# Attention, a gated FFN and an eight-expert block in one kernel: one expert's 264 rows computed with stationary weights, and score masks in quadrants

## The chip, the core and the metric

The kernel runs on one core of one Trainium2 chip. Its time is the device time of a launch in microseconds, as the median of several runs. The engines are TensorE (PE, with its weight loads as PEld), VectorE (DVE), ScalarE (ACT), GpSimd (POOL) and SyncE (SP), whose queue starts most transfers.

## What is computed

The reference, cut to what matters:

```python
# q, k, v: (4, 8, 576, 64); window 64
scores = scale * q @ k.T;  mask = (0 <= i - j < 64);  attn = softmax(where(mask, scores, -1e9))
x = attn @ v                                             # 2304 tokens x 512
x = x / sqrt(mean(x * x) + 1e-6) * rms_g
x = (silu(x @ w_gate) * (x @ w_val)) @ w_out             # 512 -> 1536 -> 512
e = argmax(x @ r_gate);  gate_w = softmax(x @ r_gate)[e];  eom = sigmoid(x @ r_eom)
out = gate_w * eom[e] * (relu(x @ w1[e]) @ w2[e])        # 8 experts, 512 -> 1024 -> 512
```

Every fp32 product outside attention is made of three products of rounded parts: high by high, high by low, low by high (`hi_i` and `lo_i` split an operand; the data type is fp32r). So a product over 512 inputs is 4 x 3 = 12 matmuls, and one over 1024 inputs is 24.

## The kernel before

**Stages.** Attention runs over 18 tiles of 128 tokens (`attention_tile`). The FFN runs over 7 parts of two or three tiles in 6 groups (`SIZES`, `GROUPS`); each group goes through the 24 slices of the hidden size, gate, value and output product (L999 to L1001, L1041 to L1043). `route` finds each token's expert and scatters its row into a table in DRAM, in which every expert has a range of its own. `experts` then runs nine blocks: a first block of 256 rows for the expert that leads before the last FFN part is done, then eight blocks, the experts in order of their number of tokens, with as many rows as `CAPS` says. What is over is left to a loop (`moe_rest`), whose number of turns is computed on the chip.

**One expert block.** `tokens` loads 128 rows at a time and transposes them (L1475). `weights` loads the expert's weights in eight parts of 512 KB into a buffer `raw` (six of these) and splits them into high and low parts (`w`). `wide` makes the first product: eight slices of the hidden size, each 12 matmuls with the weights stationary and the block's rows moving (L1544 to L1546), then relu and split (`eh`, L1550 to L1555). `block` makes the second product: for each tile of 128 rows, 24 matmuls with the hidden values stationary and 512 columns of weights moving (L1578 to L1580), so the rows come out as rows; a tile with 64 rows makes as many matmuls. The result is scaled by the token's factor (`osb`, L1589, L1591) and scattered to the output by POOL (L1596).

**The scores of one tile.** For each half j of the heads there is a result bank. A mask is laid into it first, by one matmul of `both_b` (two identities side by side) with `masks`, 512 columns (L680). A query of 64 positions looks at the 64 keys before its own and its own 64, so the mask has one triangle for each. A query that begins a sequence (4 of 36) has nothing before it: a second matmul of 256 columns adds the full mask there (L687). Then 32 matmuls of 64 x 64 add the scores (L694).

**The order of the work.** Every operation is given to a planner (`Plan`) with its cost on each engine it could run on, its buffers and a due time. `Plan.order` simulates the engines and writes one order for all of them; `SHIFT` is a list of corrections to the due times, and `K` holds the planner's settings: `SW`, the cost counted when TensorE changes between small tiles (`tiled=True`) and the whole array; `stk`, how far such work is preferred while the array is in small tiles; `warm`, until when result bank 7 of 8 is kept for filler matmuls, which keep TensorE busy in the start (L625); `vb`, `vb2` and `share`, the choice between engines. The lines in question are these:

```python
first = min((x for x in ready[e] if x[2].tiled and not x[2].done), default=None)
if first is not None and first[0] < min(x[0] for x in ready[e]) + K["stk"]:
    ...
pl.tags["bank"][7]["free"] = K["warm"]
```

Of the kernel before, what the change touches and what calls it, by code (L numbers as in the profile page):

```python
# [22 lines left out]
P = 128  # L23
# [10 lines left out]
CAPS = [128, 448, 384, 320, 256, 256, 256, 192]  # L34
SW = 0.165
# [3 lines left out]
    w_r=4, sl=1.2, n_q=4, n_kt=4, n_s=4, n_m=4, n_p=4, n_x=4, n_y=3, n_xf=1, n_val=3, pf=0.1, cold=6.0, late=1, f0=24.0, pw=110.0, pb=0.6, c1a=0, c1v=0, spe=4, lact=0, warm=38.762, wf=2.97, flead=24.233, nwv=1, port=1.0, t0=46.214, pp=93.267,  # L39
    lead=1.781, clead=9.978, stag=2.552, stage=1.001, slack=0.136, nt=2, look=-0.104, marg=-0.509, dw=1.843, ewl=3.278,  # L40
    ews=8.339, xld=43.407, xtn=7.222, mlead=14.712, vb=0.41, vb2=-0.81, tb=1165.45, share=0.149, pls=9, phs=9, sf=0, hfs=1.431, stk=305.664, rlead=7.936, span=0.317, wl=1.841,
# [46 lines left out]
]  # L88


class Buf:


    def __init__(self, tag=None, t=None):
        self.tag, self.t, self.slot = tag, t, None
# [279 lines left out]
def attention_ffn_moe(  # L375
# [291 lines left out]
    def attention_tile(t, qt, kt, al):  # L667
# [4 lines left out]
        def half(j):  # L672
            return slice(64 * j, 64 * j + 64)
# [1103 lines left out]
```

## Time and profile before

| | |
|---|---|
| median of 3 runs | 822.24 us (822.12 to 823.24) |
| the profiled execution's own time | 820.1 us |
| its span, first to last instruction | 818.4 us |
| TensorE busy | 803.6 us, 98% |
| VectorE, ScalarE, POOL busy | 473.7, 353.9, 70.2 us |
| granted TensorE clock, mean | 0.998 of full speed |

The span is what the trace covers; the time of a launch has 1.7 us around it in this execution. A matmul's busy time reaches from its start to its result, and the next one starts before that end, so the distance between two starts is what a matmul costs in a dense stretch.

### The profile page before, as it was taken

Reading aid. Unit: us, or ns where it says so; the run is one execution under the profiler, and the core shown is the slowest. Engines: PE = TensorE matmul, PEld = TensorE weight load, DVE = VectorE, ACT = ScalarE, POOL = GpSimd, SP = SyncE. Lnnn points to the kernel's source line nnn. Section 1 sums busy time; section 2 is a strip of 40 time slices with the busy share of each in tenths; the row PEclk is TensorE's granted clock in tenths of the full one; section 3 lists DMA queues with packets and bytes.
Section 4 is the critical chain, followed back from the end, with each engine's and each line's share of the span. In section 5 each row is a group of like instructions: output and inputs, shape, how many; then the busy total and the mean of one; then the engine's idle time right before and its main releaser. Section 6 shows DMA issues by size and latency. Waiting matters only on the chain.

```text
span 818.4 us, 15636 instructions
## 1 busy us (share of the span) xinstructions
PE 803.6 (98%) x5954; PEld 723.4 (88%) x5954; DVE 473.7 (58%) x1246; ACT 353.9 (43%) x990; POOL 70.2 (9%) x131
## 2 busy tenths in 40 slices
PE   9999999999999999999999999999999999999995
PEld 8888999989999898899899998899788798889993
DVE  6999999557553534632553224453465576767740
ACT  6898777547432424421642121223243323344430
POOL 2210001021101000200021001000200010111100
PEclk9999999999999999999999999999999999999999
DMA  8797979968325502632129506600594653756600
GB/s 317 260 331 246 336 291 315 297 229 314 115 104 202 191 1 68 224 124 88 52 105 356 196 2 195 228 1 1 148 291 146 215 173 121 244 165 207 205 27 20
DMA packets 54012, 146.34 MB, mean 179 GB/s; under 512 B 6800, under 2 KB 6800, under 8 KB 53936
## 3 DMA queue, kind: packets, MB, share of 16 engines
q1 hardware_dynamic: 50912, 135.48, 48.8%
q0 software_dynamic: 3024, 9.85, 3.1%
q8 instruction: 47, 0.77, 0.4%
q14 instruction: 29, 0.24, 0.1%
HBM read 120.77 MB, written 24.54 MB: 178 GB/s over the span
## 4 chain that ended last, share of the span: by engine, by line
PE 79%; issue 8%; DMA 8%; DVE 3%; ACT 1%; POOL 1%; SPq 0%; POOLq 0%; DVEq 0%
PE bank L999 12%; PE bank L1001 12%; PE bank L1000 12%; PE bank L1041 6%; PE bank L1042 6%; PE bank L1043 6%; DMA out_dram<-osb,meta 5%; PE bank L1544 2%; PE bank L1546 2%; PE bank L1545 2%; PE bank L1579 2%; PE bank L1580 2%; PE bank L1578 2%; PE bank L774 2%; PE bank L694 2%
## 5 line engine op out<-in xcount | busy, mean ns | idle before, releaser
L999 PE MATMUL bank<-xn,w 128*128 128x384 f32 (+1 forms) x672 | 215.5, 321 | 0.7 <-DVE u L1016 0.7
L1001 PE MATMUL bank<-xn,w 128*128 128x384 f32 (+1 forms) x672 | 210.4, 313 | 0.0
L1000 PE MATMUL bank<-xn,w 128*128 128x384 f32 (+1 forms) x672 | 210.3, 313 | 0.0
L999 PEld LDWEIGHTS bank<-xn,w 128*128 128x128 f32 x672 | 127.2, 189 | 5.0 <-DVE u L1016 1.0
L1000 PEld LDWEIGHTS bank<-xn,w 128*128 128x128 f32 x672 | 127.2, 189 | 1.6
L1001 PEld LDWEIGHTS bank<-xn,w 128*128 128x128 f32 x672 | 127.1, 189 | 0.0
L459 DVE TENSOR_TENSOR w<-raw,w 128x512 fp32r<-128x512 f32 x128 | 82.4, 684 | 7.4 <-ACT w L452 7.0
L1041 PE MATMUL bank<-wo,h 128*128 128x512 f32 x216 | 86.0, 398 | 0.0
L1043 PE MATMUL bank<-wo,h 128*128 128x512 f32 x216 | 84.9, 393 | 0.0
L1042 PE MATMUL bank<-wo,h 128*128 128x512 f32 x216 | 84.9, 393 | 0.0
L1016 DVE SCALAR_TENSOR_TENSOR u<-u,bank 128x384 f32<-128x384 f32 (+1 forms) x84 | 41.5, 494 | 66.8 <-ACT u L1011 66.3
L1011 ACT ACTIVATE u<-bank 128x384 f32<-128x384 f32 (+1 forms) x84 | 37.5, 446 | 94.9 <-PE bank L1001 94.0
L452 ACT CAST h<-u 128x384 fp32r<-128x384 f32 (+1 forms) x75 | 35.1, 468 | 96.4 <-DVE u L1024 96.3
L1024 DVE TENSOR_TENSOR u<-u,bank 128x384 f32<-128x384 f32 (+1 forms) x84 | 41.5, 494 | 57.8 <-PE bank L1001 57.0
L452 ACT CAST w<-raw 128x512 fp32r<-128x512 f32 x81 | 47.4, 619 | 54.8 <-DMA raw<-in_moe_w_dram 36.2
L1544 PE MATMUL bank<-xT,w 128*128 128x256 f32 (+4 forms) x224 | 68.4, 305 | 0.0
L1545 PE MATMUL bank<-xT,w 128*128 128x256 f32 (+4 forms) x224 | 68.1, 304 | 0.0
L1546 PE MATMUL bank<-xT,w 128*128 128x256 f32 (+4 forms) x224 | 68.1, 304 | 0.0
L1578 PE MATMUL bank<-w,eh 128*128 128x512 f32 (+1 forms) x168 | 66.6, 397 | 0.0
L1579 PE MATMUL bank<-w,eh 128*128 128x512 f32 (+1 forms) x168 | 66.2, 394 | 0.0
L1580 PE MATMUL bank<-w,eh 128*128 128x512 f32 (+1 forms) x168 | 66.2, 394 | 0.0
L1550 ACT ACTIVATE eh<-bank 128x256 fp32r<-128x256 f32 (+4 forms) x61 | 25.6, 420 | 68.7 <-PE bank L1546 66.6
(234 smaller groups left out, 1332.2 us busy)
## 6 DMA issues: line engine op xcount, KB each, us to landing
w<-whd SPq DMA_DIRECT2D x80, 512.0 KB, 4.5
raw<-in_moe_w_dram SPq DMA_DIRECT2D x64, 512.0 KB, 4.8
whd<-w SPq DMA_DIRECT2D x24, 512.0 KB, 5.5
val<-in_v_dram SPq DMA_DIRECT2D x18, 512.0 KB, 5.6
kt<-in_k_dram SPq DMA_DIRECT2D x18, 384.0 KB, 5.5
raw<-in_moe_w_gate_dram SPq DMA_DIRECT2D x12, 512.0 KB, 5.1
raw<-in_moe_w_val_dram SPq DMA_DIRECT2D x12, 512.0 KB, 4.0
raw<-in_moe_w_out_dram SPq DMA_DIRECT2D x12, 512.0 KB, 5.1
```

Source lines behind the costliest of these rows:

```text
L999: nc.tensor.matmul(o, lhsT=h_, rhs=xn.t[:, 0, kk], start=(kk == 0), stop=False)
L1000: nc.tensor.matmul(o, lhsT=h_, rhs=xn.t[:, 1, kk], start=False, stop=False)
L1001: nc.tensor.matmul(o, lhsT=l_, rhs=xn.t[:, 0, kk], start=False, stop=(kk == KD - 1))
L1041: nc.tensor.matmul(o, lhsT=h.t[:, 0, c], rhs=wo.t[:, 0, f], start=(n == 0), stop=False)
L1042: nc.tensor.matmul(o, lhsT=h.t[:, 0, c], rhs=wo.t[:, 1, f], start=False, stop=False)
L1043: nc.tensor.matmul(o, lhsT=h.t[:, 1, c], rhs=wo.t[:, 0, f], start=False, stop=(n == NF - 1))
L1544: nc.tensor.matmul(o, lhsT=wh, rhs=x.t[:, 0, kk, 0:N], start=(kk == 0), stop=False)
L1545: nc.tensor.matmul(o, lhsT=wh, rhs=x.t[:, 1, kk, 0:N], start=False, stop=False)
L1546: nc.tensor.matmul(o, lhsT=wl, rhs=x.t[:, 0, kk, 0:N], start=False, stop=(kk == KD - 1))
L1578: nc.tensor.matmul(bk.t[0:M], lhsT=hh, rhs=wh, start=(f == 0), stop=False)
L1579: nc.tensor.matmul(bk.t[0:M], lhsT=hh, rhs=wl, start=False, stop=False)
L1580: nc.tensor.matmul(bk.t[0:M], lhsT=hl, rhs=wh, start=False, stop=(f == NF2 - 1))
```

## The change

The block of the fourth expert in order has 264 rows, not 320. A block whose last tile has at most 32 rows (here 8) now makes its second product the other way round (`turned_block`): the weights are stationary, 128 output columns at a time, and all the block's rows move. The four results are copied out of their banks as columns by rows (into one buffer `raw` and one `t2k`), and four transposes for each tile of rows turn them back; then they are scaled and scattered as before (`weighted`, the old code as a function). The score mask is now four matmuls of 64 x 64 weights and 512 columns, one for each half of the heads and each half of the queries, and a query that begins a sequence takes its mask from other columns of `masks`, so the extra matmul is gone. The planner's settings and the whole `SHIFT` list are new.

```diff
-CAPS = [128, 448, 384, 320, 256, 256, 256, 192]
-SW = 0.165
+CAPS = [128, 448, 384, 264, 256, 256, 256, 192]
+SW = 0.06
...
-    ... warm=38.762, wf=2.97, ... slack=0.136, look=-0.104, marg=-0.509, dw=1.843, vb=0.41, vb2=-0.81, tb=1165.45, share=0.149, stk=305.664
+    ... warm=62.816, wf=1.644, ... slack=-0.04, look=-0.072, marg=-0.199, dw=1.739, vb=0.333, vb2=0.243, tb=22.485, share=-0.055, stk=0.0
...
 SHIFT = [
-    -22.3, 22, -5.8, 15.9, 30.3, 28.9, 11.1, 7.3, 39.4, -27.8, -41.3, -28, ...
...
-    both_b = fixed("both_b", [P, P], BF16)
+    both_b = fixed("both_b", [P, 64], BF16)
...
         def mmc(e):
-            for j, bk in enumerate(col):
-                nc.tensor.matmul(
-                    bk.t.rearrange("p (i g w) -> p i g w", i=4, g=2), lhsT=both_b.t[half(j)],
-                    rhs=masks.t[half(j), 0:2].unsqueeze(1).to_broadcast([64, 4, 2, 64]), start=True, stop=False,
-                )
             for c in range(2):
                 for j, bk in enumerate(col):
-                    if st[c]:
-                        nc.tensor.matmul(
-                            bk.t[half(c)].rearrange("p (i g w) -> p i g w", i=4, g=2)[:, :, 0], lhsT=both_b.t[half(j), 0:64],
-                            rhs=masks.t[half(j), 2].unsqueeze(1).to_broadcast([64, 4, 64]), start=False, stop=False,
-                        )
+                    nc.tensor.matmul(
+                        bk.t[half(c)].rearrange("p (i g w) -> p i g w", i=4, g=2), lhsT=both_b.t[half(j)],
+                        rhs=masks.t[half(j), slice(0, 3, 2) if st[c] else slice(1, 3)].unsqueeze(1).to_broadcast([64, 4, 2, 64]),
+                        start=True, stop=False,
+                    )
...
-            {"t": 1.4 + 0.3 * any(st)}, mmc, r=[qt, kt, both_b, masks], w=col, hold=halves, prio=pr + 2 * sg, tiled=True
+            {"t": 1.28}, mmc, r=[qt, kt, both_b, masks], w=col, hold=halves, prio=pr + 2 * sg, tiled=True
...
+    def turned_block(b, w, N, hs, pr):
+        yb = [Buf("raw"), Buf("t2k")]
+        def y(d):
+            return yb[0].t[:, d * N:d * N + N].bitcast(F32) if d < 3 else yb[1].t[:, 0:N]
+        for d in range(KD):
+            bk = bank()
+            for g in range(2):
+                def mm2(e, d=d, g=g, bk=bk):
+                    for f in range(4 * g, 4 * g + 4):
+                        t = ew[w, 2 + f // 4, f % 4 // 2].t
+                        wh, wl = (t[:, z, f % 2].rearrange("p k f -> p (k f)")[:, d * P:(d + 1) * P] for z in range(2))
+                        hh, hl = (hs[f][0].t[:, z, 0:N] for z in range(2))
+                        o = bk.t[:, 0:N]
+                        nc.tensor.matmul(o, lhsT=wh, rhs=hh, start=(f == 0), stop=False)
+                        nc.tensor.matmul(o, lhsT=wh, rhs=hl, start=False, stop=False)
+                        nc.tensor.matmul(o, lhsT=wl, rhs=hh, start=False, stop=(f == NF2 - 1))
+                pl.op({"t": 12 * mmt(N) + 0.02}, mm2, ..., w=[bk], prio=pr)
+                pr += 12 * mmt(N)
+            pl.op(cost(N, "hp"), lambda e, d=d, bk=bk: hi_i(e, y(d), bk.t[:, 0:N]), r=[bk], w=[(yb[d // 3], d)], prio=pr)
+        for j in range(-(-N // P)):
+            bk = bank()
+            M = min(P, N - j * P)
+            def back(e, j=j, bk=bk, M=M):
+                for d in range(KD):
+                    nc.tensor.transpose(bk.t[0:M, d * P:(d + 1) * P], y(d)[:, j * P:j * P + M], ident.t)
+            pl.op({"t": 0.43}, back, r=[*yb, ident], w=[bk], prio=pr + 0.5, rows=0.5)
+            weighted(b, j, M, bk, pr + 0.5)
+        return pr
...
     def block(b, w, N, pr):
         hs = narrow(b, w, pr) if N == P else wide(b, w, N, pr)
         pr += 6.5 if N == P else NF2 * 12 * mmt(N)
+        if 0 < N % P <= 32:
+            return turned_block(b, w, N, hs, pr)
```

## Rows read from the trace of the kernel before

**Rows 1.** The page's part 1: busy time, share of the span, instructions.

```profile
PE 803.6 (98%) x5954; PEld 723.4 (88%) x5954; DVE 473.7 (58%) x1246; ACT 353.9 (43%) x990; POOL 70.2 (9%) x131
```

**Rows 2.** Busy time by stretch: start:end, length, engines, clock, DMA share, GB/s.

```profile
core 0: us, PE busy (x) PEld busy (x) DVE busy (x) ACT busy (x) POOL busy (x), PEclk, DMA share, GB/s
0.00:20.00 20.00, 18.45 (x312) 16.00 (x313) 12.46 (x40) 12.43 (x59) 4.84 (x31) 1.00 0.88 315
40.00:60.00 20.00, 19.69 (x202) 17.82 (x199) 19.55 (x53) 19.43 (x57) 2.08 (x2) 1.00 0.91 334
560.00:600.00 40.00, 37.63 (x250) 32.19 (x249) 17.28 (x77) 13.34 (x31) 5.08 (x7) 1.00 0.43 129
677.50:726.50 49.00, 49.00 (x291) 42.95 (x290) 31.99 (x69) 18.35 (x36) 5.10 (x5) 1.00 0.56 179
```

**Rows 3.** The same for the filler matmuls alone (L625), until 41.4 us.

```profile
0.00:41.40 41.40, 16.48 (x216) 14.97 (x216) 1.00 0.81 289
```

**Rows 4.** What TensorE waited for: us in total, times, longest.

```profile
PE bank L1475 <- DMA t2k<-xs: 1.6, 1, 1.6
...
PE bank L1475 <- DMA xs<-xs: 0.7, 2, 0.4
```

**Rows 5.** Timeline of TensorE, expert stage: start, busy time, instruction; stretches of one width.

```profile
682.53 0.31 PE L1544 MATMUL bank<-xT,w 128*128 128x320 f32 x1
...
686.06 0.40 PE L1578 MATMUL bank<-w,eh 128*128 128x512 f32 x1
...
688.86 0.31 PE L1544 MATMUL bank<-xT,w 128*128 128x320 f32 x1
...
738.95 0.28 PE L1545 MATMUL bank<-xT,w 128*128 128x256 f32 x1
...
744.51 0.39 PE L1578 MATMUL bank<-w,eh 128*128 128x512 f32 x1
...
784.83 0.28 PE L1545 MATMUL bank<-xT,w 128*128 128x192 f32 x1
...
787.40 0.42 PE L1578 MATMUL bank<-w,eh 128*128 128x512 f32 x1
```

**Rows 6.** The same timeline: four transposes, and the matmul behind them.

```profile
677.53 0.60 PE L1475 MATMUL bank<-ident,xs 128*128 128x128 f32 x4
677.88 0.39 PE L1544 MATMUL bank<-xT,w 128*128 128x320 f32 x1
```

**Rows 7.** Groups of instructions by shape: evictions behind the first product.

```profile
L1550 ACT ACTIVATE eh<-bank 128x256 fp32r<-128x256 f32 x29 | 11.2, 385 | 25.0 <-PE bank L1546 23.7 <-PE bank L1280 1.2
L1550 ACT ACTIVATE eh<-bank 128x320 fp32r<-128x320 f32 x8 | 3.5, 438 | 12.2 <-PE bank L1546 12.1
...
L1555 DVE SCALAR_TENSOR_TENSOR eh<-bank,eh 128x256 fp32r<-128x256 f32 x32 | 13.2, 420 | 11.8 <-ACT eh L1550 11.7
```

**Rows 8.** The page's part 6: loads of expert weights, KB, us to landing.

```profile
raw<-in_moe_w_dram SPq DMA_DIRECT2D x64, 512.0 KB, 4.8
```

**Rows 9.** Timeline of TensorE: two score groups; the first begins a sequence.

```profile
28.91 0.39 PE L680 MATMUL bank<-masks,both_b 64*128 64x512 bf16 x2
...
30.33 0.32 PE L851 MATMUL bank<-ident,y 128*128 128x128 f32 x1
...
75.13 0.39 PE L1043 MATMUL bank<-wo,h 128*128 128x512 f32 x1
75.45 0.39 PE L680 MATMUL bank<-masks,both_b 64*128 64x512 bf16 x2
75.77 1.10 PE L694 MATMUL bank<-kt,q 64*64 64x128 f32 x32
76.81 0.39 PE L999 MATMUL bank<-xn,w 128*128 128x256 f32 x1
77.03 0.28 PE L1000 MATMUL bank<-xn,w 128*128 128x256 f32 x1
```

**Rows 10.** Timeline of TensorE between the last FFN matmul and the first big block.

```profile
564.21 0.39 PE L1043 MATMUL bank<-wo,h 128*128 128x512 f32 x1
...
592.37 0.66 PE L1475 MATMUL bank<-ident,t2k 128*128 128x128 f32 x4 [1.62 <-DMA t2k<-xs]
```

More of the change, by code (lines that the diff above doesn't have):

```diff
@@ L38 @@
 K = dict(
-    w_r=4, sl=1.2, n_q=4, n_kt=4, n_s=4, n_m=4, n_p=4, n_x=4, n_y=3, n_xf=1, n_val=3, pf=0.1, cold=6.0, late=1, f0=24.0, pw=110.0, pb=0.6, c1a=0, c1v=0, spe=4, lact=0, warm=38.762, wf=2.97, flead=24.233, nwv=1, port=1.0, t0=46.214, pp=93.267,
-    lead=1.781, clead=9.978, stag=2.552, stage=1.001, slack=0.136, nt=2, look=-0.104, marg=-0.509, dw=1.843, ewl=3.278,
-    ews=8.339, xld=43.407, xtn=7.222, mlead=14.712, vb=0.41, vb2=-0.81, tb=1165.45, share=0.149, pls=9, phs=9, sf=0, hfs=1.431, stk=305.664, rlead=7.936, span=0.317, wl=1.841,
+    w_r=4, sl=1.2, n_q=4, n_kt=4, n_s=4, n_m=4, n_p=4, n_x=4, n_y=3, n_xf=1, n_val=3, pf=0.1, cold=6.0, late=1, f0=24.0, pw=110.0, pb=0.6, c1a=0, c1v=0, spe=4, lact=0, warm=62.816, wf=1.644, flead=24.233, nwv=1, port=1.0, t0=46.214, pp=93.267,
+    lead=1.781, clead=9.978, stag=2.552, stage=1.001, slack=-0.04, nt=2, look=-0.072, marg=-0.199, dw=1.739, ewl=3.278,
+    ews=8.339, xld=43.407, xtn=7.222, mlead=14.712, vb=0.333, vb2=0.243, tb=22.485, share=-0.055, pls=9, phs=9, sf=0, hfs=1.431, stk=0.0, rlead=7.936, span=0.317, wl=1.841,
 )
 SHIFT = [
[42 rows of a table removed]
[42 rows of a table added]
 ]
@@ L518, in c_masks @@
             r = slice(64 * c, 64 * c + 64)
-            a = masks.t[r, 0]
+            a = masks.t[r, 1]
             nc.gpsimd.affine_select(
@@ L522, in c_masks @@
             )
-            a = masks.t[r, 1]
+            a = masks.t[r, 2]
             nc.gpsimd.affine_select(
@@ L529, in c_zero @@
         nc.vector.memset(ident.t, 0.0)
-        nc.vector.memset(masks.t[:, 0:2], 0.0)
-        nc.vector.memset(masks.t[:, 2], NEG)
+        nc.vector.memset(masks.t[:, 1:3], 0.0)
+        nc.vector.memset(masks.t[:, 0], NEG)
     def c_ones(e):
@@ L548, in c_both @@
     def c_both(e):
-        nc.vector.tensor_tensor(out=both_b.t[:, 0:64], in0=ident.t[:, 0:64], in1=ident.t[:, 64:P], op=ALU.add)
-        nc.vector.tensor_tensor(out=both_b.t[:, 64:P], in0=ident.t[:, 0:64], in1=ident.t[:, 64:P], op=ALU.add)
-    pl.op({"v": 0.28}, c_both, r=[ident], w=[both_b], prio=-97)
+        nc.vector.tensor_tensor(out=both_b.t, in0=ident.t[:, 0:64], in1=ident.t[:, 64:P], op=ALU.add)
+    pl.op({"v": 0.14}, c_both, r=[ident], w=[both_b], prio=-97)
     made = pl.op({"v": 0.4}, c_ones, w=[ones, ones_b, tri, seed_b], prio=-98)
@@ L1563, in wide @@
         return hs
+    def turned_block(b, w, N, hs, pr):
[14 more added lines that the diff above has]
+                        nc.tensor.matmul(o, lhsT=wl, rhs=hh, start=False, stop=(f == NF2 - 1))
+                pl.op(
+                    {"t": 12 * mmt(N) + 0.02}, mm2, r=[ew[w, 2 + g, hf] for hf in range(2)] + [h for h, _ in hs[4 * g:4 * g + 4]],
+                    w=[bk], prio=pr,
+                )
+                pr += 12 * mmt(N)
[9 more added lines that the diff above has]
+        return pr
@@ new lines, in weighted, with scaled, put @@
+    def weighted(b, j, M, bk, pr):
+        o, m = Buf("osb"), meta[b, j]
+        def scaled(e):
+            if e == "a":
+                nc.scalar.activation(out=o.t[0:M], in_=bk.t[0:M], func=AF.Copy, scale=m.t[0:M, 1:2])
+            else:
+                nc.vector.tensor_scalar(out=o.t[0:M], in0=bk.t[0:M], scalar1=m.t[0:M, 1:2], scalar2=None, op0=ALU.mult)
+        def put(e):
+            nc.gpsimd.indirect_dma_start(
+                out=out, out_offset=bass.IndirectOffsetOnAxis(ap=m.t[0:M, 0:1].bitcast(I32), axis=0),
+                in_=o.t[0:M], in_offset=None, bounds_check=NT - 1, oob_is_err=False,
+            )
+        pl.op({"a": 0.55, "v": 0.61}, scaled, r=[bk, m], w=[o], prio=pr)
+        puts.append(pl.op({"p": 1.0}, put, r=[o, m], dma=0.73, prio=pr, after=puts[-1:]))
@@ L1584, in block @@
                 pr += 2.78
-            o, m = Buf("osb"), meta[b, j]
-            def scaled(e, bk=bk, o=o, m=m, M=M):
-                if e == "a":
-                    nc.scalar.activation(out=o.t[0:M], in_=bk.t[0:M], func=AF.Copy, scale=m.t[0:M, 1:2])
-                else:
-                    nc.vector.tensor_scalar(
-                        out=o.t[0:M], in0=bk.t[0:M], scalar1=m.t[0:M, 1:2], scalar2=None, op0=ALU.mult
-                    )
-            def put(e, o=o, m=m, M=M):
-                nc.gpsimd.indirect_dma_start(
-                    out=out, out_offset=bass.IndirectOffsetOnAxis(ap=m.t[0:M, 0:1].bitcast(I32), axis=0),
-                    in_=o.t[0:M], in_offset=None, bounds_check=NT - 1, oob_is_err=False,
-                )
-            pl.op({"a": 0.55, "v": 0.61}, scaled, r=[bk, m], w=[o], prio=pr)
-            puts.append(pl.op({"p": 1.0}, put, r=[o, m], dma=0.73, prio=pr, after=puts[-1:]))
+            weighted(b, j, M, bk, pr)
         return pr
@@ L1612, in experts @@
             todo.append((b, w, n, at, at + NF2 * c1))
-            at += NF2 * c1 + -(-n // P) * 2 * 2.78
+            at += NF2 * c1 + (8 * 12 * mmt(n) + 1.3 if 0 < n % P <= 32 else -(-n // P) * 2 * 2.78)
         done_w = set()
```

84 rows, old and new, of the table SHIFT are left out of this document.

## The prediction

> **What bounds the kernel now.** I read the busy shares first, then the stretches, then what TensorE waited for, and last its instructions in order of time. TensorE is busy 98% of the span, VectorE 58%, ScalarE 43%, and it has a weight load for every matmul [rows 1]. But a matmul's busy time runs past the start of the next one, so I judge by start-to-start distances. By stretches: in the first 20 us TensorE has gaps and shares the time with 216 filler matmuls that end before 41.4 us [rows 2, 3]; from 40 to 60 us it is nearly gapless, with VectorE at 19.55 and ScalarE at 19.43 of 20 us; from 560 to 600 us it lacks 2.4 us; in the 49 us around the block that is changed it has no gap at a granted clock of 1.00, while VectorE is busy 32 us and ScalarE 18 [rows 2]. All waits that the trace gives to TensorE's matmuls in the expert stage are 1.6 + 0.7 us, for the loads behind the last scatter [rows 4]. So after the start the time is the sum of TensorE's start-to-start distances, and what is taken from that sum in the expert stage comes off the end.
>
> **The block of 264 rows: first product.** It stays 8 x 12 = 96 matmuls, with 264 moving columns for 320. At 320 columns, 24 matmuls start between 682.53 and 686.06 us, 0.147 us each; at 512, 12 between 686.06 and 688.86, 0.233 each; at 256, 47 between 738.95 and 744.51, 0.118 each; at 192, 23 between 784.83 and 787.40, 0.112 each [rows 5]. From 256 to 320 that is 0.00045 us a column, so 264 columns give an estimated 0.122 us; the bounds are 0.118 (as 256) and 0.147 (as 320), and 264 is nearest to 256. Saved: 96 x (0.147 - 0.122) = 2.4 us (0 to 2.8).
>
> **Second product, turned.** Removed: three token tiles of 24 matmuls with 512 columns; the last of them holds 64 rows and costs as much as a full one. 72 x 0.233 = 16.8 us. Added: four column tiles of the output, 24 matmuls each, 264 columns, with the weights stationary: 96 x 0.122 = 11.7 us (11.3 to 14.1). Each matmul has its own weight load before and after; that load is of the kind that the 256-column rows already carry. Added too: the way back, three groups of four transposes. Such a group takes 0.35 us, and the matmul behind it starts late by 0.24 - 0.147 = 0.09 us [rows 6], so 0.44 us a group, 1.3 us in all. The last group has 8 rows and may be cheaper; I leave it at that. Net: 16.8 - 11.7 - 1.3 = 3.8 us saved (1.4 to 4.2).
>
> **What goes beside it.** Four evictions of 264 columns are new. The nearest rows are 0.385 us on ScalarE and 0.420 on VectorE for 256 columns [rows 7]: 1.7 us in all. The eight pairs of evictions after the first product shrink from 0.438 us at 320 columns (ScalarE's half) towards 0.385, 0.4 us on either engine. Both engines have over 15 of 49 us free there [rows 2], so this costs nothing as long as the transposes back are queued behind another block's matmuls; if they are not, the last eviction is bare, about 0.5 us. The turned output takes one of six buffers into which weights are loaded, and one of the two small ones, for some 10 us. Weight parts come one in 2.8 us (eight to a block of 256 rows, 96 x 0.118 + 48 x 0.233 = 22.5 us), and land in 4.8 us [rows 8]; five buffers then allow 14 us a part, landing included. The scatters keep their count, three, and POOL does little else there (5.1 us of 49).
>
> **Masks in quadrants.** Before, a tile's mask takes two matmuls, each on 64 rows and 128 columns of the array, and the 32 score matmuls behind them use tiles of 64 x 64. In the steady stage the mask starts at 75.45 us, the scores at 75.77, the next work at 76.81 [rows 9]: 0.32 us for the mask, though one matmul of 512 columns paces at 0.233. So about 0.1 us is lost where the tile's shape changes. A like amount is lost going in (75.13 + 0.233 against 75.45) and coming out (0.22 to the second matmul against 0.118). After, the four mask matmuls have the scores' shape. If the four run at once, as the scores do (32 matmuls in 1.04 us, 0.033 each, where a whole-array matmul of as many fp32 columns takes 0.35 / 4 = 0.088 [rows 6, 9]), the change of shape between mask and scores goes: 0.1 us a tile. The Trainium skill (TensorEngine Tiling (Array Packing), Key Properties) says that a change of tiling mode, not of tile, drains the engine; the 0.32 us agrees, and by that rule one drain of three goes at each tile. The four tiles that begin a sequence also lose their extra matmuls: mask and scores take 1.42 us there (28.91 to 30.33) for 1.36, so 0.06 us each [rows 9]. Four of the 18 tiles run in the start, where fillers take up what is saved. I take 14 x 0.1 + 3 x 0.06 = 1.6 us. Below that nothing may come (the drain stays); the worst case is a rival. At the head, one VectorE instruction less is hidden behind the first loads.
>
> **The new plan.** All due times change, so the order on every engine does. One setting is plain: work in small tiles is no longer preferred when the array is in that mode. Two such groups back to back save the way out and in, 0.19 us; at most 9 pairs, so 0 to 1.7 us lost; I take 0.5. The last of TensorE's eight result banks is kept for fillers until 62.8 us of the plan, for 38.8; see the rivals. Otherwise I count the plan at zero, both signs open.
>
> **Sum.** 820.1 us of the profiled execution - 2.4 - 3.8 - 1.6 + 0.5 = 812.8 us. The median of the runs, 822.24, lies 2.1 us above that execution, so 814.9 for the median. A difference under 0.2% (1.6 us) is about what this kernel's runs can't tell from none. The forecast's own range, from the bounds: 812.5 to 819.
>
> **Rivals.**
> 1. *The plan gives part back* (16%). Two places. The last FFN matmul starts at 564.21 and the first tokens of the big blocks reach TensorE at 592.37; in between only the first block of 256 rows (22.5 us) and the last routing cover, and 2.4 us stay bare already [rows 2, 10]. Whatever of that block is ordered earlier opens the wait by as much. And with a bank fewer from 38.8 to 62.8 us, where four banks hold sums and four are left for all else, up to a quarter of 24 us = 6 us could go. Typical: 3 us, 818; with 6 us, 821. Against it: the planner counts banks and waits itself, and this stretch is bound by VectorE and ScalarE as well [rows 2]. Only above 7.3 us does it turn the sign.
> 2. *The plan also gains* (10%): the 2.4 us at 590 and some of the 16.5 us of fillers before 41.4 us [rows 3, 4] go. 811 to 812.
> 3. *The four masks run one after another* (4%): slower. Place: the score group of 18 tiles. Four at 0.233 are 0.93 us for 0.32, so 0.61 x 18 = 11 us lost against 6.2 - 0.5 saved: about 827.5. It decides the sign from 0.32 us a tile on. For it: no row here has four such matmuls of 512 columns. Against it: the score rows, whose matmuls would take 2.8 us if whole-array pacing held, and take 1.04 [rows 6, 9].
> 4. *Narrow matmuls pay a fixed price* (4%): between 192 and 256 columns the distance moves by only 0.006 us, so below some width the columns no longer set it. If that held 264 at 0.147, the block would save 16.8 - 14.1 - 1.3 = 1.4 us and the sum be 819.7. Against it: the row at 256 columns, on the near side, paces at 0.118 [rows 5]. The Trainium skill (TensorE: Matmul & The Clock Gate, Back-to-back issue gap) speaks against the change: it gives a sustained 81 ns a matmul at 128 columns and 131 at 512. By a line between these (an estimate from that page) 264 columns take 0.099 us, 96 matmuls 9.5 us against 9.4 for the 72 removed, and the turned product loses the 1.3 us of transposes; the rows disagree, with 0.118 at 256 and 0.233 at 512 [rows 5].
> 5. *The block does not hold its tokens* (2%): were there more than 264, the loop that follows the planned part would run once: eight weight parts that land in 4.8 us each [rows 8], two buffers deep, 19 us or more, so 834 and up. The reference's inputs send 258 tokens to that expert by my count, and none of that loop's matmuls shows before, so only a miscount would do it.
>
> **Chances.** Forecast 64%, rivals 16, 10, 4, 4, 2. Faster by over 0.2%: 64 + 10 + 10 of the first rival + 2 of the fourth = 86%; within 0.2%: 3 + 2 = 5%; slower: 3 of the first rival, 4 and 2 = 9%. Range 810.5 to 819.5: it takes the forecast's range, the second rival and the lighter half of the first, and leaves out the rest, some 2 in 10.
>
> **What would show it.** Right: matmuls of 264 columns 0.12 to 0.125 us apart in both products; four groups of 24 in the turned one, three groups of transposes at 0.35 to 0.45 us; four mask matmuls starting together and the scores 0.2 to 0.25 us behind them; TensorE's last matmul some 7 us earlier in the span, and the same work behind it. Wrong: a gap of over 3 us between the last FFN matmul and the big blocks; TensorE waiting at 40 to 63 us or for turned results; more fillers behind 41 us; a mask of over 0.3 us; a matmul from the loop behind the planned part.

## The result, and the profile after

| | before | after |
|---|---|---|
| median of the runs | 822.22 us (822.12 to 823.24) | 814.68 us (812.85 to 816.35) |
| the profiled execution: time, span | 820.1, 818.4 us | 815.9, 813.9 us |
| TensorE's last matmul starts | 809.15 us | 804.60 us |

The ratio of the medians is 0.9905 (0.9878 to 0.9932). The forecast was 814.9 us. A second measurement of the same kernel, in five rounds, gave 814.15 us and 0.9902 (0.9885 to 0.992); its profiled execution took 815.3 us. So the median fell by some 8 us, while the profiled executions lie only 4 to 5 us apart: the one of before is near the fast end of its runs, both of after lie above the medians of theirs. What a part is worth is read below from medians, and from traces only stretch by stretch.

The page of the kernel after, part 1, as in [rows 1]:

```profile
PE 798.6 (98%) x6050; PEld 723.1 (89%) x6050; DVE 471.1 (58%) x1262; ACT 355.0 (44%) x993; POOL 59.6 (7%) x103
```

Busy time by stretch (columns as in [rows 2]) and what TensorE waited for, as in [rows 4]:

```profile
40.00:60.00 20.00, 19.97 (x192) 18.66 (x193) 19.33 (x49) 17.42 (x56) 1.77 (x2) 1.00 0.84 282
560.00:600.00 40.00, 39.43 (x264) 33.92 (x263) 19.55 (x79) 13.46 (x32) 5.04 (x7) 1.00 0.38 124
677.00:725.00 48.00, 46.53 (x342) 43.71 (x342) 27.00 (x62) 20.76 (x44) 5.47 (x5) 1.00 0.53 174
```

```profile
PE bank L1538 <- DVE eh L1549: 1.5, 2, 1.1
PE bank L993 <- DVE u L1010: 1.3, 1, 1.3
...
PE bank L1591 <- DVE eh L1549: 0.4, 1, 0.4
...
PE bank L1469 <- DMA xs<-xs: 0.2, 1, 0.2
```

The reader sees what moved. Of the 2.4 us that TensorE lacked from 560 to 600 us in [rows 2], 0.6 is left, and the waits for the scatter's loads (now L1469) have shrunk to 0.2 us. In their place stand 1.3 us at the end of the FFN (L993; 0.7 us before), 1.5 us behind the changed block, where before there was no gap, and 0.45 us at 773 us, two blocks on. The TensorE timeline of the changed block:

```profile
693.98 0.28 PE L1538 MATMUL bank<-xT,w 128*128 128x264 f32 x1
...
699.74 1.47 PE L1469 MATMUL bank<-ident,xs 128*128 128x128 f32 x12
700.97 0.37 PE L1575 MATMUL bank<-eh,w 128*128 128x264 f32 x1
...
709.83 0.28 PE L1538 MATMUL bank<-xT,w 128*128 128x256 f32 x1
...
712.67 0.49 PE L1591 MATMUL bank<-ident,raw 128*128 128x128 f32 x3
...
713.64 0.55 PE L1591 MATMUL bank<-ident,raw 128*128 128x128 f32 x3 [0.38 <-DVE eh L1549]
...
714.58 0.39 PE L1538 MATMUL bank<-xT,w 128*128 128x256 f32 x1
...
722.86 0.39 PE L1632 MATMUL bank<-w,eh 128*128 128x512 f32 x1
724.34 0.39 PE L1538 MATMUL bank<-xT,w 128*128 128x256 f32 x1 [1.09 <-DVE eh L1549]
```

48 matmuls of the first product in 5.76 us, 0.120 each; 72 of the turned one from 700.97 to 709.83, 0.123 each, for 0.149 at 320 columns and 0.232 for the 512 columns that they replace. The transposes back begin 24 matmuls behind the turned product, so the copies out are covered, and take 1.9 us to 714.58 with a wait of 0.38 in between.

A score group of after (answering [rows 9]), and a pair of groups of before that [rows 9] does not show:

```profile
255.45 0.41 PE L680 MATMUL bank<-masks,both_b 64*64 64x512 bf16 x4
255.69 1.04 PE L688 MATMUL bank<-kt,q 64*64 64x128 f32 x32
256.67 0.45 PE L993 MATMUL bank<-xn,w 128*128 128x384 f32 x1
```

```profile
388.64 0.34 PE L1001 MATMUL bank<-xn,w 128*128 128x384 f32 x1
388.91 0.39 PE L680 MATMUL bank<-masks,both_b 64*128 64x512 bf16 x2
...
390.27 0.39 PE L680 MATMUL bank<-masks,both_b 64*128 64x512 bf16 x2
...
391.62 0.50 PE L1041 MATMUL bank<-wo,h 128*128 128x512 f32 x1
391.95 0.39 PE L1042 MATMUL bank<-wo,h 128*128 128x512 f32 x1
```

The scores start 0.24 us behind the masks, for 0.32, and a group takes 1.22 us, for 1.36; the tiles that begin a sequence take 1.21 too, for 1.42. Two groups back to back took 2.71 us before, twice 1.355; what lies in front of them and behind them they pay once and not twice (below).

### The profile page after: what moved, and what is told of

Read it like the earlier page. It is cut to its first block, busy times and chain, and to the rows that moved or that the text cites. A ratio compares the mean times of both kernels' runs of the same rounds, so it can differ in the third digit from the quotient of the medians.

```text
span 813.9 us, 15811 instructions
## 1 busy us (share of the span) xinstructions
PE 798.6 (98%) x6050; PEld 723.1 (89%) x6050; DVE 471.1 (58%) x1262; ACT 355.0 (44%) x993; POOL 59.6 (7%) x103
## 4 chain that ended last, share of the span: by engine, by line
PE 78%; issue 9%; DMA 6%; DVE 4%; SPq 1%; ACT 1%; POOL 0%; POOLq 0%; ACTq 0%; DVEq 0%
PE bank L993 11%; PE bank L995 10%; PE bank L994 10%; PE bank L1035 5%; PE bank L1036 5%; PE bank L1037 5%; PE bank L1538 3%; PE bank L1540 3%; PE bank L1539 3%; DMA raw<-in_moe_w_dram 3%; PE bank L1630 3%; PE bank L1632 3%; PE bank L1631 3%; PE bank L768 2%; PE bank L751 2%
## 5 line engine op out<-in xcount | busy, mean ns | idle before, releaser
L993 PE MATMUL bank<-xn,w 128*128 128x384 f32 (+1 forms) x672 | 215.2, 320 | 1.3 <-DVE u L1010 1.3
L994 PE MATMUL bank<-xn,w 128*128 128x384 f32 (+1 forms) x672 | 210.1, 313 | 0.0
L993 PEld LDWEIGHTS bank<-xn,w 128*128 128x128 f32 x672 | 127.2, 189 | 6.2 <-DVE u L1010 1.7
L1010 DVE SCALAR_TENSOR_TENSOR u<-u,bank 128x384 f32<-128x384 f32 (+1 forms) x84 | 41.4, 494 | 88.4 <-ACT u L1005 88.0
L1538 PE MATMUL bank<-xT,w 128*128 128x256 f32 (+4 forms) x224 | 68.0, 304 | 1.5 <-DVE eh L1549 1.5
L1540 PE MATMUL bank<-xT,w 128*128 128x256 f32 (+4 forms) x224 | 67.3, 300 | 0.0
L1539 PE MATMUL bank<-xT,w 128*128 128x256 f32 (+4 forms) x224 | 67.2, 300 | 0.0
L1630 PE MATMUL bank<-w,eh 128*128 128x512 f32 (+1 forms) x144 | 57.3, 398 | 0.0
L1632 PE MATMUL bank<-w,eh 128*128 128x512 f32 (+1 forms) x144 | 56.7, 394 | 0.0
L1631 PE MATMUL bank<-w,eh 128*128 128x512 f32 (+1 forms) x144 | 56.7, 394 | 0.0
```

What stands on the lines that cost most here:

```text
L993: nc.tensor.matmul(o, lhsT=h_, rhs=xn.t[:, 0, kk], start=(kk == 0), stop=False)
L994: nc.tensor.matmul(o, lhsT=h_, rhs=xn.t[:, 1, kk], start=False, stop=False)
L1538: nc.tensor.matmul(o, lhsT=wh, rhs=x.t[:, 0, kk, 0:N], start=(kk == 0), stop=False)
L1539: nc.tensor.matmul(o, lhsT=wh, rhs=x.t[:, 1, kk, 0:N], start=False, stop=False)
L1540: nc.tensor.matmul(o, lhsT=wl, rhs=x.t[:, 0, kk, 0:N], start=False, stop=(kk == KD - 1))
L1630: nc.tensor.matmul(bk.t[0:M], lhsT=hh, rhs=wh, start=(f == 0), stop=False)
```

## The experiments

Medians are of each kernel's runs; ratios are to the kernel before on the same chip (822.55, 821.6 and 822.62 us in the three sessions). A kernel "in the order of before" gives every engine the instruction order of before (with the turned block, up to that block: there and just behind it some evictions and weight splits change place or engine), so its stretches can be compared one by one.

**The block alone**: `CAPS` with 264, `turned_block` and `weighted`, in the code of before, settings, corrections and the due times of all other work kept.

```diff
-CAPS = [128, 448, 384, 320, 256, 256, 256, 192]
+CAPS = [128, 448, 384, 264, 256, 256, 256, 192]
+        if 0 < N % P <= 32:
+            return turned_block(b, w, N, hs, pr)
```

> The kernel before with the block part alone: 264 rows, turned second product; masks, settings and due-time corrections of before, and all due times of the other blocks kept. Theory A: the 6.2 us of the block come off, so 816 (815 to 817.5). Theory B (the new plan made the gain, the turned block loses by bare evictions and by the buffer it takes from the weight loads): 819.5 to 823.

815.04 us (814.15 to 816.22), 0.9915 (0.9898 to 0.9931). So 7.0 us (5.7 to 8.4), and no TensorE wait behind 593 us: the forecast 6.2 is within.

**The rows alone**: 264 rows in the code of before, nothing turned, planned as if they were 320.

```diff
-CAPS = [128, 448, 384, 320, 256, 256, 256, 192]
+CAPS = [128, 448, 384, 264, 256, 256, 256, 192]
+        PN = 320 if b == 3 else N
-            pl.op(cost(N, "hp"), relu, r=[bk], w=[(h, 0)], prio=pr)
+            pl.op(cost(PN, "hp"), relu, r=[bk], w=[(h, 0)], prio=pr)
```

> The kernel before with 264 rows for 320 in the fourth expert's block, nothing turned, its order unchanged. Theory (a matmul of 264 columns paces at 0.120 to 0.122 us, one of 320 at 0.147): 96 x 0.026 = 2.5 us, so 819.7 beside 822.2. Rival (the whole gain of the block, 7 us with the turn, comes from the turn): no change, 822.

818.37 us (817.29 to 820.67), 0.9959 (0.9946 to 0.9973): 3.4 us (2.2 to 4.4): the 2.5 of the pace lies within, nothing does not. The turn takes the rest of the 7.0, 3.6 us.

**The masks alone**: `c_masks`, `c_both` and the mask matmuls of after in the code and the order of before.

```diff
-                    bk.t.rearrange("p (i g w) -> p i g w", i=4, g=2), lhsT=both_b.t[half(j)],
-                    rhs=masks.t[half(j), 0:2].unsqueeze(1).to_broadcast([64, 4, 2, 64]), start=True, stop=False,
+                        bk.t[half(c)].rearrange("p (i g w) -> p i g w", i=4, g=2), lhsT=both_b.t[half(j)],
+                        rhs=masks.t[half(j), slice(0, 3, 2) if st[c] else slice(1, 3)].unsqueeze(1).to_broadcast([64, 4, 2, 64]),
```

> The kernel before with the four-quadrant masks alone, and the planner's cost for the group left at its old number, so that the order of all work is that of before. Theory A (one change of tile shape goes at each tile): 0.1 us in each of the 14 tiles behind the start and a little for the tiles that begin a sequence, 1.4 to 2.0 us, so about 820.5. Rival (the change of shape is paid elsewhere): no change, 822. Rival (the four run one after another): 827 and more.

818.72 us (817.51 to 822.47), 0.9963 (0.9946 to 0.9979): 3.0 us (1.7 to 4.4), above theory A's 1.4 to 2.0, which the interval still reaches. The timeline of the pair in this kernel:

```profile
277.02 0.34 PE L995 MATMUL bank<-xn,w 128*128 128x384 f32 x1
277.29 0.41 PE L680 MATMUL bank<-masks,both_b 64*64 64x512 bf16 x4
...
278.41 0.39 PE L680 MATMUL bank<-masks,both_b 64*64 64x512 bf16 x4
...
279.60 0.50 PE L1035 MATMUL bank<-wo,h 128*128 128x512 f32 x1
279.93 0.39 PE L1036 MATMUL bank<-wo,h 128*128 128x512 f32 x1
```

2.31 us for the pair: 1.12 and 1.19, 0.1 us less than twice the 1.21 of a group alone. With the masks of before the pair took no less than twice a group.

**The masks back**: the changed kernel, order unchanged, with the masks of before.

```diff
-                        bk.t[half(c)].rearrange("p (i g w) -> p i g w", i=4, g=2), lhsT=both_b.t[half(j)],
+                    bk.t.rearrange("p (i g w) -> p i g w", i=4, g=2), lhsT=both_b.t[half(j)],
+                    rhs=masks.t[half(j), 0:2].unsqueeze(1).to_broadcast([64, 4, 2, 64]), start=True, stop=False,
```

> The changed kernel with the masks of before (two matmuls of 512 columns, and the extra one for tiles that begin a sequence), planner's cost unchanged, so that the order of all work is that of the changed kernel. Theory A, with the mask term as the run in the order of before measured it (3 us, where the forecast had 1.6 to 2): 817 to 818, that is 0.994 of the kernel before. Rival (that run's 3 us came from something else, the group itself gives 0.1 us a tile): 815.5 to 816.

817.76 us (817.04 to 820.82), 0.995 (0.9933 to 0.9966), beside 0.9902 for the changed kernel: 3.9 us for the masks, as theory A has it; the two intervals leave 1 to 7.

**The plan alone**: the code of before, 320 rows and old masks, with the settings and corrections of after.

```diff
-SW = 0.165
+SW = 0.06
-K = dict(..., warm=38.762, ..., stk=305.664, ...)
+K = dict(..., warm=62.816, ..., stk=0.0, ...)
```

> The kernel before (320 rows, second product not turned, masks of before) with the planner's settings and due-time corrections of the changed kernel. Theory A (the plan is worth nothing by itself): 821 to 824. Theory C (the new plan gives 2 us back that the two code parts had earned): 824 to 826. Theory B (the new plan gains by itself): 817 to 820.

823.39 us (822.88 to 825.48), 1.0026 (1.0011 to 1.004): 2.1 us slower, and within the range of theory A.

**The changed code under the old plan**: settings and corrections of before, due times as in the block's experiment, the new cost of a mask.

> The changed kernel with the planner's settings and due-time corrections of before, and the due times of the other blocks as before: both code parts, not the new plan. Theory A (the plan is worth nothing by itself): 814 to 815.5, as the changed kernel. Theory B (the new plan is needed for the gain): 817 or more. Theory C (the new plan gives a part back): 812 to 814.

818.34 us (815.93 to 819.34), 0.9952 (0.9933 to 0.9971): theory B by its number, which the next run does not bear out.

**Both parts in the order of before**: the block's kernel above with the new masks, at the masks' old cost.

> The block part in the plan of before, and the new masks in the same order, the planner's cost for the group left at its old number. If the two parts add up as measured alone (7.0 and 3.0 us): 812 to 813, 0.988 of before, and the new plan gives some 2 us back. If they do not add up (as with the settings of before and the new cost, 818): 815 or more, and the masks' gain is lost elsewhere once the block is shorter.

814.74 us (814.3 to 815.25), 0.9911 (0.9882 to 0.994), the same as the changed kernel. The parts measured alone would make 10 us, this run gives 7.3 (4.9 to 9.7). Beside the one before it here, this kernel has the same code, planned with another cost for the mask. The order of the work, the engine of some operations (VectorE 1244 instructions for 1249, ScalarE 995 for 999) and the number of fillers (216 for 252) follow from that; the medians lie 3.6 us apart, though the intervals overlap a little.

**An own buffer for the turned result**, in place of `raw`, in the changed kernel.

```diff
-        yb = [Buf("raw"), Buf("t2k")]
+        yb = [Buf("yy"), Buf("t2k")]
```

> The changed kernel with a buffer of its own for the turned output, not one of the six that weights are loaded into; the planner orders the work anew around it. If the taken buffer makes the next block's weights late (TensorE waits 1.5 to 1.9 us behind the turned block, for relu results that stand behind weight splits): those waits go, 812 to 813. Rival (the waits come from the order, not from the buffer): they stay or move, 814 to 816.

815.16 us (812.99 to 817.0), 0.9913 (0.9885 to 0.9942): no gain that shows. In its trace the next weight load starts at 708.34 us, not at 713.28 as in the changed kernel, so the buffer does seem to hold loads back, but TensorE still waits 0.67 us at the transposes and 0.53 at 770 us (0.38 and 0.45 in the changed kernel). The same execution lost some 1.6 us to the clock in the FFN (last section), so its whole time says little about the buffer.

**Bank 7 free early**, in the changed kernel.

```diff
-K = dict(..., warm=62.816, ...)
+K = dict(..., warm=38.762, ...)
```

> The changed kernel with result bank 7 free at 38.8 us of the plan, as before, not at 62.8. The order follows from the planner and so moves elsewhere too. The prediction's theory (a bank counts for little there): within 1 us of the changed kernel's 814.2 to 814.7. Rival: the 38 fillers that now lie between 40 and 62.8 us (2.6 us busy) stand in for work that found no bank; then 811.5 to 812.

817.52 us (817.04 to 817.85), 0.9946 (0.9927 to 0.9965): some 3 us slower, against both expectations. The fillers of the changed kernel, then of this one (in bank 7, and in other banks), with first and last start:

```profile
L624 PE MATMUL warm<-ones_b x248: 219/219/314, 1.2 to 44.1; 128*128 128x128 bf16 x124
```

```profile
L624 PE MATMUL warm<-ones_b x206: 218/219/312, 1.2 to 39.6; 128*128 128x128 bf16 x103
L624 PE MATMUL bank<-ones_b x48: 219/219/231, 41.8 to 94.7; 128*128 128x128 bf16 x48
```

With the bank free, fillers went on in the other banks, 254 in all for 248. So this run changes the order and leaves the fillers, and does not price the bank by itself. TensorE waits 2.6 us for `u` (L993) and 1.3 for `x` (L680) here, where the changed kernel waited 1.3 for `u` and not for `x`.

**Not turned**: the changed kernel with the second product of before, 264 rows, corrections kept for all other work.

```diff
-        if 0 < N % P <= 32:
-            return turned_block(b, w, N, hs, pr)
```

> The changed kernel with its second product not turned: three tiles of 24 matmuls with 512 columns as before, 264 rows, the corrections to the due times kept for all other work. Theory: the turn saves 16.8 - 11.7 - 1.3 = 3.8 us, so 818.0 to 818.5 beside the changed kernel's 814.2 to 814.7. Rival: the 1.5 us that TensorE waits around the turned product and the 3 us of transposes with what is bare behind them eat most of it: under 1.5 us, 815.7.

816.23 us (815.68 to 817.97), 0.9929 (0.991 to 0.9948). In medians the turn is worth 2.2 us here, between the two expectations and just clear of noise. From the last transposes of `t2k` (L1469 of after) to the last matmul the traces show 217.3 us for 214.9, 2.4 us; without TensorE's waits in that stretch, 1.2 and 2.1 us, it is 3.4. So the turn itself keeps most of its worth, and the changed kernel has 0.9 us more of waits.

**Five sizes narrowed**, on the kernel with both parts in the order of before.

```diff
-CAPS = [128, 448, 384, 264, 256, 256, 256, 192]
+CAPS = [128, 440, 376, 264, 240, 240, 232, 192]
+PLANNED = {440: 448, 376: 384, 240: 256, 232: 256}
```

> The block and the masks in the order of before, with seven sizes narrowed on top: 448 to 440 rows, 384 to 376, 256 to 240 twice and 256 to 232, each block planned with its old width, so the order stands. Only the first products get narrower: 96 matmuls for each size. Theory that the columns set the pace at every width (0.00045 us a column between 256 and 320): 72 columns x 96 = 6912, times 0.00045 = 3.1 us off the 814.7 of both parts in the old order, so 811.6. Rival, a floor under some width: between 192 and 256 the distance moves by 0.0001 us a column, so the three narrow sizes give 56 x 96 x 0.0001 = 0.5 us and the two wide ones 0.7, 1.2 us in all: 813.5.

810.6 us (810.05 to 810.95), 0.9859 (0.9834 to 0.9884): better than both kernels, 4 us below the one that it starts from and past both expectations. (The text counts seven sizes; those it lists are five.) Its TensorE timeline, 36 matmuls of 240 columns and then 36 of 232:

```profile
745.79 0.27 PE L1542 MATMUL bank<-xT,w 128*128 128x240 f32 x1
...
749.84 0.27 PE L1542 MATMUL bank<-xT,w 128*128 128x232 f32 x1
...
753.86 0.40 PE L1634 MATMUL bank<-w,eh 128*128 128x512 f32 x1
```

0.1125 and 0.1117 us each. Over the whole stage the mean start-to-start distances are 0.111 at 192 columns, 0.112 at 232, 0.114 at 240, 0.1187 at 256, 0.173 at 376, 0.175 at 384, 0.201 at 440, 0.205 at 448. So the five sizes save 96 x (0.004 + 0.002 + 2 x 0.0045 + 0.007) = 2.1 us. Of the rest, the profiled executions show 2.9 us as waits and a slow stretch of its parent's that this kernel has not to that extent (below), against 1.0 us of new waits for `eh`.

## Why the prediction came out right, point by point

**The block: right, place and size.** In kernels with the order of before, the time from TensorE's last transposes of `t2k` (L1475 of before) to its last matmul is one and the same work but for the edit (with the masks, their gain lies ahead of it):

| order of before, with | last transposes of `t2k` | last matmul | between |
|---|---|---|---|
| nothing (before) | 592.8 | 809.15 | 216.4 |
| 264 rows | 592.3 | 806.34 | 214.1 |
| 264 rows, turned | 593.1 | 803.20 | 210.1 |
| masks | 590.6 | 808.17 | 217.6 |
| masks, 264 rows, turned | 591.5 | 804.15 | 212.6 |
| the same, five sizes narrowed | 590.3 | 799.79 | 209.5 |

The rows give 2.3 us (forecast 2.4), the turn 4.0 (forecast 3.8); without the waits in the first three stretches (0.8, 0.6 and 0.2 us) they give 2.2 and 3.5. Rival 4, a fixed price that would hold 264 columns at 0.147, is refuted by the 0.120 to 0.124; a floor exists, but lower: 0.111 at 192 columns and 0.112 at 232. The Trainium skill's figures for a sustained matmul (TensorE: Matmul & The Clock Gate, Back-to-back issue gap), by which the turned product would have lost, are not what these rows show, 0.123 at 264 columns and 0.232 at 512: the turn gained.

**The masks: the right mechanism, mis-sized.** The term was 14 x 0.1 + 3 x 0.06 = 1.6 us. The traces show 0.14 for each of the 14 tiles outside the start and 0.07 more for the three that begin a sequence there: 2.2 us. The change of shape that goes was taken as 0.1; it is 0.14. The medians give more, 3.0 alone, with 1.7 as the lower end, and 3.9 in the changed kernel. There the traces can place it: with what lies in front of them, the groups outside the start take 2.9 us less than with the masks back, and 1.06 of this falls in the one pair of that order, at 173 us (3.67 us for 4.73), which stalls within its scores in both kernels. Rival 3, four masks one after the other, did not come: 0.24 us for all four.

**The lost preference for small tiles: about as counted.** It was put at 0.5 us lost, 0.19 for a pair. Beyond the pace of its neighbours (0.233 and 0.118 us), a single group of before costs 1.55 us, from 75.13 to 77.03 [rows 9]. The pair, from 388.64 to 391.95 beyond 0.175 and 0.233, costs 2.90, so 0.2 us less than two single ones: the way in and out is paid once. With the new masks it is 2.50 us for a pair (277.02 to 279.93) and 1.41 for a group, so 0.3 us saved, as no mask on 64 x 128 stands between the two groups of scores in 64 x 64. The Trainium skill (TensorEngine Tiling (Array Packing), Key Properties) has a change of tiling mode drain the engine; the pairs agree. The order of before has three pairs, the new one has one: two pairs fewer, 0.4 to 0.6 us. Whether the one setting does it, or the rest of the new plan, no run separates.

**The plan at zero: wrong on the code of before, open on the changed code.** On the code of before the new plan costs 2.1 us. On the changed code it stands 0.1 to 0.6 us below the order of before, which can't be told from none. But the kernel with five sizes narrowed keeps that order too and gains 11.6 us, of which its columns give 2.1; that leaves 9.5 for both parts, near the 10 of the parts alone, and by it the new plan takes back some 1.5 us. The traces show where those two kernels part: at the scatter's loads, behind the first block. First the block alone, then block and masks, then the same with five sizes narrowed, all in the order of before, TensorE:

```profile
590.90 0.40 PE L1640 MATMUL bank<-w,eh 128*128 128x512 f32 x1
592.70 0.66 PE L1477 MATMUL bank<-ident,t2k 128*128 128x128 f32 x4 [1.40 <-DMA t2k<-xs]
593.47 1.36 PE L1477 MATMUL bank<-ident,xs 128*128 128x128 f32 x8
...
596.49 0.40 PE L1506 MATMUL bank<-w,xT 128*128 128x512 f32 x1
```

```profile
589.30 0.40 PE L1634 MATMUL bank<-w,eh 128*128 128x512 f32 x1
591.14 0.66 PE L1471 MATMUL bank<-ident,t2k 128*128 128x128 f32 x4 [1.44 <-DMA t2k<-xs]
592.63 0.63 PE L1471 MATMUL bank<-ident,xs 128*128 128x128 f32 x4 [0.83 <-DMA xs<-xs]
593.71 1.00 PE L1471 MATMUL bank<-ident,xs 128*128 128x128 f32 x4 [0.45 <-issue]
...
597.40 0.39 PE L1500 MATMUL bank<-w,xT 128*128 128x512 f32 x1
```

```profile
588.53 0.40 PE L1636 MATMUL bank<-w,eh 128*128 128x512 f32 x1
589.95 0.66 PE L1472 MATMUL bank<-ident,t2k 128*128 128x128 f32 x4 [1.02 <-DMA t2k<-xs]
590.97 1.24 PE L1472 MATMUL bank<-ident,xs 128*128 128x128 f32 x8 [0.36 <-DMA xs<-xs]
...
593.73 0.39 PE L1501 MATMUL bank<-w,xT 128*128 128x512 f32 x1
```

From the last matmul of the first block to the eighth of 512 columns behind these transposes it is 5.6 us, 8.1 and 5.2. In the other traces in this order it is 6.2 (before), 5.7 (264 rows) and 5.7 (masks alone). So the masks do not make this place longer. In the one execution with 8.1 us, TensorE waits 0.83 + 0.45 us more, and then seven matmuls from 594.36 us take 3.04 us (to 597.40), where those of the first kernel take 1.73 (594.76 to 596.49), at a lower clock (last section): 0.83 + 0.45 + 1.31 = 2.6 us, as much as the 212.6 - 210.1 by which this stretch is longer. Why its loads came late is open, and so is how often that happens.

The new order has 0.2 us of waits for the scatter's loads, so the first place of rival 1 did not come and rival 2's gain did. It pays elsewhere: 0.6 us more at L993, the waits behind the block, and a stall in its one pair of score groups:

```profile
174.53 1.35 PE L688 MATMUL bank<-kt,q 64*64 64x128 f32 x29
176.15 0.45 PE L688 MATMUL bank<-kt,q 64*64 64x128 f32 x3 [0.28 <-issue]
```

From its mask at 173.20 us to the next work the pair takes 3.67 us (3.69 in the second measurement), where two single groups take 2.43: 1.2 us. With the new plan on the code of before it takes 4.79, where pairs of the old plan take 2.7 to 2.9: some 2 us, the size of that run's whole loss. What stalls it the profile does not show ("issue" is time in which the engine waited for nothing that it shows).

The second place of rival 1, the bank kept until 62.8 us, does not show as a cost: from 40 to 60 us TensorE is busy 19.97 of 20 us, with the last filler at 44.1. These fillers (34 behind 41 us) are one of the prediction's signs of being wrong, and cost nothing that shows.

**No gap around the block: wrong in both profiled executions.** The sum counted on a TensorE without waits there. VectorE's timeline in the kernel after, then in the one with the masks back, which has the same order:

```profile
709.85 0.15 DVE L1462 COPY meta<-xs 128x1 int32<-128x1 int32 x1 [4.54 <-DMA xs<-xs]
...
713.18 0.41 DVE L1549 SCALAR_TENSOR_TENSOR eh<-bank,eh 128x256 fp32r<-128x256 f32 x1
...
722.04 0.58 DVE L456 CAST w<-raw 128x512 fp32r<-128x512 f32 x1 [3.49 <-DMA raw<-in_moe_w_dram]
...
723.86 0.75 DVE L1549 SCALAR_TENSOR_TENSOR eh<-bank,eh 128x256 fp32r<-128x256 f32 x2
```

```profile
722.31 0.43 DVE L456 CAST w<-raw 128x512 fp32r<-128x512 f32 x1 [0.70 <-DMA raw<-in_moe_w_dram]
```

At 709.85 VectorE has sat 4.54 us for token rows; weight splits come next in its order, then the split `eh` at 713.18, and TensorE, at 713.64, waits 0.38 us for what that split releases (1.5 us in the second measurement); the turned results were copied out by 710.4. At 722.04 it has sat 3.49 us for weights, with the next `eh` behind them, and TensorE waits 1.09 us at 724.34. With the masks of before TensorE comes to this point some 3 us later, the weights land at nearly the same time (722.3), and no TensorE wait over 0.1 us is left from 589 to 800 us: its stretch from the last transposes of `t2k` to the end is 212.5 us, for 214.9. So 2.4 of the 3.5 us that the masks had put TensorE ahead were given back in these two executions, 2.1 of them in waits for loads and for what stands behind loads. The medians, 3.6 us apart, do not show it, so how often it is paid is open. The buffer may have its part: with an own one the load starts 5 us earlier, VectorE waits 0.74 us for it and the wait at 724 is gone; but 0.7 us at the transposes and 0.5 at 770 us remain, and no gain shows in the median. That the taken `raw` costs nothing, as the prediction counted, is thus neither shown nor refuted. Which transfer would have to come earlier for the whole of it was not tried.

In sum: the block came as counted, the masks gave 0.6 to 2.3 us more, and waits that were counted at nothing, with a new plan that costs up to 2 us, took about that back; of this, the traces place 1.5 us behind the block and 1.2 in the stalled pair. The mechanism of the two parts was right; that the median is met to 0.2 us is luck, as these cancel. In the profiled executions TensorE's last matmul is only 4.6 us earlier (5.1 in the second), not the 7 that the prediction named as a sign: they hold these waits, and the stall at 173 us.

## What to carry over

Time a part in the old instruction order as well as in the new one, and before a wait in one trace is called the effect of an edit, look at the same place in another kernel with the same edit: 8.1 us in one execution were 5.2 and 5.7 in the others. A saved microsecond can be lost again at the next wait for something that does not move with it; ask what each one meets next. Where matmuls carry their own weight loads, fewer columns pay down to the measured floor (0.111 us; 240 columns still take 0.114): swapping the operands pays when a short last tile would cost a full pass, and narrowing five blocks by 8 to 24 rows saved 2.1 us by their columns.

## What the hardware showed unasked

**The clock after a wait.** In the kernel with both parts in the order of before, TensorE made 12 transposes between 589.6 and 594.4 us and waited 1.44 + 0.83 + 0.45 = 2.7 us in between. Its granted clock then stood at 0.50 of full speed, the lower of the two levels, as the busy times by stretch show (the clock is the third number from the end):

```profile
595.00:596.00 1.00, 1.00 (x4) 0.81 (x3) 0.63 (x2) 0.34 (x1) 0.00 (x0) 0.50 0.78 240
...
598.00:599.00 1.00, 1.00 (x8) 0.75 (x6) 0.00 (x0) 0.19 (x1) 0.00 (x0) 1.00 0.80 262
```

In the kernel before, with 1.62 + 0.44 + 0.31 = 2.4 us of waits in the same place, it stayed at 1.00. The kernel with an own buffer shows the lower level too, from 529.5 to 532.9 us, behind a dense stretch and one wait of 1.92 us; a wait of 1.73 us there in the second measurement of the changed kernel left the clock at 1.00:

```profile
529.45 0.67 PE L994 MATMUL bank<-xn,w 128*128 128x384 f32 x1 [1.92 <-DVE u L1011]
...
533.03 0.34 PE L996 MATMUL bank<-xn,w 128*128 128x384 f32 x1
```

The 11 matmuls from the one to the other take 3.58 us, 0.32 each, where they take 0.175 at 1.00: some 1.6 us lost. So waits of 2.7 and 1.9 us cost 1.3 and 1.6 us more behind their end.

**Neighbours in small tiles.** Two score groups that stand together pay the way into small tiles and out of them once: 0.2 us saved with masks on 64 x 128, 0.3 us with masks that have the scores' tile shape.
